# A fused attention and two-MLP kernel: the combined first weight stored with both parts side by side through one slotted tile, two attention units with longer query and key runs, and a new table of priorities

## The chip, the cores and the metric

The kernel runs on one core of a Trainium2 chip. A core has TensorE (matmuls; PE in the rows, its weight loads PEld), VectorE (DVE), ScalarE (ACT), GpSimd (POOL) and SyncE (SP), which here only issues transfers; 16 DMA engines carry them. The metric is the device time of one execution in microseconds, lower being better. Three runs of the kernel before took 761.55, 761.88 and 757.69 us, median 761.55.

## What is computed

Three parts follow each other, all in float32, with 4 batches of 576 tokens, 8 heads of 64 and a model width of 512.

```python
# attention: a coarse one on means over 4 tokens, repeated 4 times, plus a local one
out_d = sm_attn(mean4(q), mean4(k), mean4(v))
mask = np.abs(pos[:, None] - pos[None, :]) < 4
scores = np.where(mask, scale * q @ k.T, -1e9)
attn_out = np.repeat(out_d, 4, axis=2) + softmax(scores) @ v
# first MLP (w_k: 512x1024, w_v: 1024x512, w_r: 512x512), x_prev: x one token earlier
xk = mu_k * x + (1 - mu_k) * x_prev;  xr = mu_r * x + (1 - mu_r) * x_prev
x1 = sigmoid(xr @ w_r) * (np.maximum(xk @ w_k, 0) ** 2 @ w_v)
# second MLP (w_ch1: 512x2048, w_ch2: 2048x512)
xn = (x1 - mean) / np.sqrt(var + 1e-6) * g_ln
out = x1 + np.maximum(xn @ w_ch1, 0) @ w_ch2
```

The weights arrive as float64; each is read as pairs of 32-bit words and put together on the chip.

## The kernel before

**Precision.** Every large product is made of three matmuls on a high and a low part of each operand (`mm3`, L794 to L796): high times high, high times low, low times high. So each operand is split: a cast to the high part (`copy`, L391 on ScalarE or L392 on VectorE), then a subtraction for the low part (VectorE or POOL). A weight tile of 128x512 is loaded by `load_f32` (L405, 512 KB into a `w64` buffer, of which there are two), takes two passes on ScalarE (L411, L413) and two on VectorE (L418, L422), and is then split.

**Attention.** 16 units of two heads each; four units make a batch. A unit loads its queries and keys in one of several modes, set by `m0` to `m15` of the table: mode 0 with 128-byte runs (L508), modes 1 and 3 with two loads of 256-byte runs for each of q and k (L500), mode 2 with one load of 1536-byte runs for each (L493). In modes 1 to 3 TensorE turns the rows (tq, L571 to L577). Then come scores (sc, L645), the coarse scores (ds, L671), softmax on VectorE and ScalarE, transposes (tp, L723), the coarse output (up, L734) and the local output (pv, L764), and the sum into xT (L778), from which the first MLP takes its tokens. Values come in tiles v and vw (L517, L531).

**First MLP.** Six chunks of 384 tokens. For a chunk `prep` mixes neighbouring tokens and splits (tmu, xrh, xrl, xkh, xkl), `moe_r` makes the gate (psum tile psr, weights wr), `moe_k` the hidden columns (psk, weights wk) and `accumulate` the output (psv, weights wv). The chunks run between and after the attention units.

**Second MLP.** Three pairs of chunks. Each pair is a 2x2 block product by a Strassen-like scheme of seven products, for which the first weight is combined beforehand: `w1_combine` (L926) runs four times (two column groups g, two row blocks j), adds and subtracts quarter tiles a, and `put` (L938) splits each of the seven sums and stores high and low part to a scratch tensor s_dram. Before the change `put` takes for every part a buffer of its own: for g = 0 the seven tags sa1 to sa7 in turn, for g = 1 three tags alt0 to alt2 (L942); each part is stored by its own transfer (L950), 256 KB in runs of 512 bytes. Later `m2_product` (L1090) loads a 256 KB tile of s_dram for each product (sa, L1093); the first pair has a buffer for each of the seven products, the later pairs a ring of eleven (`ring`, L1183: seven sa tags and four wa), which they share with the tiles ta of the second weight (t_dram, L1365). The second weight is combined in `w2_combine` on tiles t (L903, L907). The normalised tokens go through z_dram and come back as zb (L1019), which VectorE transposes into raw (L1025); raw is summed and split into xn (L1082). Hidden columns of the later pairs are q (L1270 to L1288), split into hh and hl (L391, L903), and multiplied into pso.

**What sets the order.** The kernel is recorded as operations with an engine or a choice of engines, a cost, a priority and the buffers that they read and write. `Plan.order` gives each engine, step by step, the operation that can start first, by priority among equals; all engines and the SP queue then work in that order. The priorities, and the penalties `dve` and `pool` that tilt the choice between engines, come from the table PRM. Where TensorE is left without work before the first psv tile exists, warm-up matmuls (L449) are put in, one for each 0.14 us of the planner's own time.

## Time and profile before

| | before |
|---|---|
| profiled execution | 760.96 us, span 759.0 us |
| TensorE busy | 741.1 us (98%), 6248 matmuls |
| VectorE busy | 609.6 us (80%) |
| ScalarE busy | 466.5 us (61%) |
| POOL busy | 101.2 us (13%) |
| DMA | 180.33 MB, 81.6% of 16 engines in the core's queue |
| granted TensorE clock | full in all 40 slices |

Busy time of TensorE counts overlapping matmuls: one matmul stands with its latency (about 340 ns for 384 columns), and the next starts before it ends. A short wait can hide under that. A group's idle time is that of the engine just before its instructions, put down to what ended it.

### The profile page before, as it was taken

How to read it: one execution, taken by the hardware profiler on the slowest of the kernel's cores; microseconds unless marked ns; L12 is line 12 of the kernel's file. 1: busy time of each engine (PE TensorE's matmuls, PEld its weight loads, DVE VectorE, ACT ScalarE, POOL GpSimd, SP SyncE). 2: the span in 40 equal slices, each digit the busy share in tenths (PEclk: the TensorE clock that was granted, in tenths of full speed). 3: DMA queues.
4: the chain of work that ended last, by engine and by line, in shares of the span. 5: the costliest groups of instructions: out<-in, count | busy, mean ns of one | idle time of the engine just before them, and what ended most of it. 6: DMA issues, size and time to landing. Idle time of an engine off the chain costs nothing.

```text
span 759.0 us, 17473 instructions
## 1 busy us (share of the span) xinstructions
PE 741.1 (98%) x6248; PEld 659.9 (87%) x6248; DVE 609.6 (80%) x1304; ACT 466.5 (61%) x1073; POOL 101.2 (13%) x155
## 2 busy tenths in 40 slices
PE   9989999999999999999999999999989999999998
PEld 6767878888778888887988889989989999999998
DVE  6899999998985877978798698978578996334986
ACT  5788998987876766958853265452347452443552
POOL 3001112212100000001021022230101112110101
PEclk9999999999999999999999999999999999999999
DMA  9999696788585997883479979999997888986684
GB/s 185 180 199 187 166 198 135 164 176 172 171 190 188 279 309 222 232 271 122 126 252 364 268 255 354 352 341 334 310 321 237 244 253 282 382 255 205 210 263 154
DMA packets 198817, 180.33 MB, mean 238 GB/s; under 512 B 91968, under 2 KB 139468, under 8 KB 198732
## 3 DMA queue, kind: packets, MB, share of 16 engines
q1 hardware_dynamic: 198732, 179.23, 81.6%
q8 instruction: 50, 0.82, 0.5%
q14 instruction: 35, 0.29, 0.1%
HBM read 134.09 MB, written 45.09 MB: 236 GB/s over the span
## 4 chain that ended last, share of the span: by engine, by line
PE 73%; DMA 10%; DVE 8%; ACT 6%; issue 2%; SPq 0%; POOL 0%; DVEq 0%; POOLq 0%; ACTq 0%
PE pso L796 8%; PE pso L795 8%; PE pso L794 8%; PE psh L794 6%; PE psh L795 6%; PE psh L796 6%; PE psk L794 4%; PE psk L796 3%; PE psk L795 3%; DMA zb<-z_dram 3%; PE psv L794 3%; PE psv L796 3%; PE psv L795 3%; DMA w<-in_moe_w_k_dram 2%; PE warm L449 1%
## 5 line engine op out<-in xcount | busy, mean ns | idle before, releaser
L794 PE MATMUL psh<-xn,sa 128*128 128x384 f32 x336 | 114.2, 340 | 3.4 <-ACT q L1288 1.5
L795 PE MATMUL psh<-xn,sa 128*128 128x384 f32 x336 | 113.0, 336 | 0.0
L796 PE MATMUL psh<-xn,sa 128*128 128x384 f32 x336 | 112.8, 336 | 0.0
L391 ACT CAST hh<-q 128x384 fp32r<-128x384 f32 x109 | 56.2, 516 | 49.3 <-PE pso L795 44.2
L796 PE MATMUL pso<-ta,hl 128*128 128x256 f32 x300 | 84.6, 282 | 0.0
L795 PE MATMUL pso<-ta,hh 128*128 128x256 f32 x300 | 84.4, 281 | 0.0
L794 PE MATMUL pso<-ta,hh 128*128 128x256 f32 x300 | 84.2, 281 | 0.0
L794 PEld LDWEIGHTS psh<-xn,sa 128*128 128x128 f32 x336 | 63.0, 188 | 9.6 <-DVE c L1145 2.0
L795 PEld LDWEIGHTS psh<-xn,sa 128*128 128x128 f32 x336 | 63.1, 188 | 2.1
L796 PEld LDWEIGHTS psh<-xn,sa 128*128 128x128 f32 x336 | 63.1, 188 | 0.0
L903 DVE TENSOR_TENSOR hl<-q,hh 128x384 fp32r<-128x384 f32 x93 | 51.4, 557 | 9.6 <-ACT hh L391 8.5
L796 PEld LDWEIGHTS pso<-ta,hl 128*128 128x128 f32 x300 | 56.7, 189 | 0.0
L794 PEld LDWEIGHTS pso<-ta,hh 128*128 128x128 f32 x300 | 56.5, 188 | 0.0
L795 PEld LDWEIGHTS pso<-ta,hh 128*128 128x128 f32 x300 | 56.4, 188 | 0.0
L1288 ACT ACTIVATE q<-q 128x384 f32<-128x384 f32 x48 | 25.1, 525 | 45.6 <-DVE q L1278 24.5
L903 POOL TENSOR_TENSOR hl<-q,hh 128x384 fp32r<-128x384 f32 x19 | 19.8, 1047 | 152.8 <-ACT hh L391 152.7
L395 ACT ACTIVATE kr<-psk 128x384 f32<-128x384 f32 x46 | 22.4, 486 | 25.8 <-PE psk L796 23.9
L859 DVE TENSOR_TENSOR kl<-kr,kh 128x384 fp32r<-128x384 f32 x43 | 23.8, 554 | 17.4 <-ACT kr L858 17.0
L413 ACT ACTIVATE w<-w 128x512 uint32<-128x512 uint8 x52 | 34.9, 671 | 0.0
L907 DVE TENSOR_TENSOR q<-q,q 128x384 f32<-128x384 f32 x60 | 34.2, 577 | 0.0
L411 ACT ACTIVATE wf<-w 128x512 f32<-128x512 f32 x36 | 24.2, 672 | 16.1 <-DMA w<-in_moe_w_k_dram 5.3
L818 DVE SCALAR_TENSOR_TENSOR tmu<-xT,oms,tmu 128x384 f32<-128x384 f32 (+1 forms) x64 | 31.8, 513 | 2.7 <-ACT tmu L812 2.6
(585 smaller groups left out, 2103.4 us busy)
## 6 DMA issues: line engine op xcount, KB each, us to landing
sa<-s_dram SPq DMA_DIRECT2D x168, 256.0 KB, 4.6
ta<-t_dram SPq DMA_DIRECT2D x100, 256.0 KB, 3.2
w<-in_moe_w_ch_dram SPq DMA_DIRECT2D x32, 512.0 KB, 5.2
s_dram<-s SPq DMA_DIRECT2D x56, 256.0 KB, 4.0
t_dram<-t SPq DMA_DIRECT2D x32, 256.0 KB, 5.6
vw<-in_v_dram SPq DMA_DIRECT2D x62, 96.0 KB, 4.0
x_dram<-r SPq DMA_DIRECT2D x18, 256.0 KB, 2.7
x1t<-x_dram SPq DMA_DIRECT2D x6, 768.0 KB, 5.8
```

Of the source, the lines that this page charges most:

```text
L391: return [("ACT", c_act(n), lambda: nc.scalar.copy(dst(), src()), False), ("DVE", c_dve(n, True), lambda: nc.vector.tensor_copy(dst(), src ...
L395: return [("ACT", c_act(n, True), lambda: nc.scalar.activation(dst(), src(), AF.Relu), False), ("DVE", c_dve(n), lambda: nc.vector.tensor_ ...
L411: add("ACT", c_act(512), prio, lambda: nc.scalar.activation(f(), w64().bitcast(F32)[:, :, 1], AF.Abs, scale=2.0 ** -112), r=[w64], w=[f])
L413: add("ACT", c_act(512), prio, lambda: nc.scalar.activation(w64()[:, :, 0], w64().bitcast(U8).rearrange("p a (b c) -> p a b c", c=4)[:, :, ...
L794: nc.tensor.matmul(ps, lh, rh, start=start, stop=False, skip_group_check=more)
L795: nc.tensor.matmul(ps, lh, rl, start=False, stop=False, skip_group_check=more)
L796: nc.tensor.matmul(ps, ll, rh, start=False, stop=stop, skip_group_check=more)
L818: lambda t=t, o=o, n=n, prv=prv, kt=kt: nc.vector.scalar_tensor_tensor(t()[:, o:o + n], prv(), om[:, kt:kt + 1], t()[:, o:o + n], op0=ALU. ...
L859: add(either(C, lambda e: e.tensor_tensor(kl(), kr(), kh().bitcast(F32), op=ALU.subtract)), 0, prio, None, r=[kr, kh], w=[kl])
L903: add(either(n, lambda e: e.tensor_tensor(lo(), src(), hi().bitcast(F32), op=ALU.subtract)), 0, prio, None, r=r + wh, w=wl)
L907: add(either(n, lambda e: e.tensor_tensor(out(), a(), b(), op=op))[skip:], 0, prio, None, r=r, w=w)
L1288: return [("ACT", c_act(n), lambda: nc.scalar.activation(t(), t(), AF.Relu), False), ("DVE", c_dve(n, True), lambda: nc.vector.tensor_scal ...
```

## The change

1. The combined first weight goes through one tile `sring` of seven slots of 2 KB a partition. A `put` takes two neighbouring slots (three such pairs in turn, for both column groups), writes high and low part interleaved by 128 columns, and stores both with one transfer of 512 KB in runs of 1024 bytes. The sa tiles of the second MLP, and seven of the eleven places of the ring, become slots of the same tile.
2. Units 1 and 4 change from mode 1 to mode 2.
3. Nearly all other numbers of PRM are replaced. Two latencies of the planner become entries of the table, with the values that they had.

```diff
 PRM = dict(
-    thin=89.915, t0=-16.294, t1=-9.875, t2=6.158, t3=7.667, t4=48.796, t5=19.99, t6=6.382, t7=-23.592, t8=-0.47,
-    t9=-5.238, t10=-2.702, t11=0.12, t12=5.747, t13=-8.176, t14=-15.681, t15=-4.758, m0=2, m1=1, m2=0, m3=3, m4=1,
+    thin=89.915, t0=-1.975, t1=-8.717, t2=-1.015, t3=-1.866, t4=56.342, t5=38.532, t6=12.477, t7=24.291, t8=11.675,
+    t9=-14.459, t10=-2.748, t11=-6.438, t12=10.757, t13=10.235, t14=-8.667, t15=-6.125, m0=2, m1=2, m2=0, m3=3, m4=2,
...
-    n_put = [0, 0]
+    n_put = [0]
+    sring = Buf(w1tiles, [P, 7, 512], F32R, "sring", 1)
+
+    def slot(k, shape):
+        return View(sring, k, lambda t: t[:, k].rearrange("p (a b) -> p a b", b=shape[-1]) if len(shape) == 3 else
+                    t[:, k].rearrange("p (a b c) -> p a b c", b=shape[2], c=shape[3]))
...
         def put(i, src):
-            parts = []
-            for x in range(2):
-
-                tag = f"sa{n_put[0] % 7 + 1}" if g == 0 else f"alt{n_put[1] % 3}"
-                n_put[g] += 1
-                parts.append(Buf(w1tiles, [P, 512], F32R, tag, 1, f"s{i}"))
-            hi, lo = parts
-            add(copy(512, hi, src), 0, prio, None, r=[src], w=[hi])
-            add(either(512, lambda e: e.tensor_tensor(lo(), src(), hi().bitcast(F32), op=ALU.subtract)), 0, prio, None,
+
+            k = n_put[0] % 3
+            n_put[0] += 1
+            both = lambda t: t[:, 2 * k:2 * k + 2].rearrange("p a b -> p (a b)").rearrange(
+                "p (f x c) -> p f x c", x=2, c=P)
+            hi, lo = (View(sring, 2 * k + x, lambda t, x=x: both(t)[:, :, x]) for x in range(2))
+            raw = lambda: src().rearrange("p (f c) -> p f c", c=P)
+            add(copy(512, hi, raw), 0, prio, None, r=[src], w=[hi])
+            add(either(512, lambda e: e.tensor_tensor(lo(), raw(), hi().bitcast(F32), op=ALU.subtract)), 0, prio, None,
                 r=[src, hi], w=[lo])
-            for x, b in enumerate(parts):
-                add("SP", c_dma(P * 2048, 512), prio, lambda x=x, b=b: nc.sync.dma_start(
-                    out=s_dram[4 * g:4 * g + 4, SEQ.index(i), :, j, x].rearrange("f p c -> p f c"),
-                    in_=b().bitcast(F32).rearrange("p (f c) -> p f c", c=P)), r=[b], w=[(sd, (i, g, j, x))], lat=2.2)
+            add("SP", c_dma(P * 3000), prio, lambda: nc.sync.dma_start(
+                out=s_dram[4 * g:4 * g + 4, SEQ.index(i), :, j].rearrange("f p x c -> p f (x c)"),
+                in_=both(sring()).bitcast(F32).rearrange("p f x c -> p f (x c)")), r=[hi, lo],
+                w=[(sd, (i, g, j, x)) for x in range(2)], lat=2.2)
...
-        s = ring([P, 2, 2, P], "sa") if kept else Buf(w1tiles, [P, 2, 2, P], F32R, f"sa{i}", 1)
+        s = ring([P, 2, 2, P], "sa") if kept else slot(SEQ.index(i), [P, 2, 2, P])
...
-        return Buf(w1tiles, shape, F32R, *((f"sa{SEQ[k]}", 1) if k < 7 else ("wa", 4)), name)
+        return slot(k, shape) if k < 7 else Buf(w1tiles, shape, F32R, "wa", 4, name)
```

How the new table moves instructions is seen at three places. Lines are one to six higher in the changed kernel. The first place is the head of SP's queue (w_ are the w64 buffers, in_moe_w_k_dram and in_moe_w_r_dram the weights, kin and qin keys and queries, vraw the three vectors). Before:

```order
L405 DMA w_157<-in_moe_w_r_dram 128x1024
L493 DMA kin<-in_k_dram 96x2x384
L493 DMA qin<-in_q_dram 96x2x384
L405 DMA w_175<-in_moe_w_r_dram 128x1024
L500 DMA kin<-in_k_dram 96x6x64 x2
L500 DMA qin<-in_q_dram 96x6x64 x2
L1422 DMA vraw<-in_moe_mu_k_dram 4x128
L1422 DMA vraw<-in_moe_mu_r_dram 4x128
L1422 DMA vraw<-in_moe_g_ln_dram 4x128
```

After:

```order
L406 DMA w_157<-in_moe_w_k_dram 128x1024
L406 DMA w_171<-in_moe_w_k_dram 128x1024
L1428 DMA vraw<-in_moe_mu_k_dram 4x128
L1428 DMA vraw<-in_moe_mu_r_dram 4x128
L1428 DMA vraw<-in_moe_g_ln_dram 4x128
L494 DMA kin<-in_k_dram 96x2x384
L494 DMA qin<-in_q_dram 96x2x384
L494 DMA kin<-in_k_dram 96x2x384
L494 DMA qin<-in_q_dram 96x2x384
```

Two w_k weights and the vectors now stand ahead of unit 0's keys, where one w_r weight stood, and unit 1's keys and queries are one long-run load each. The four w_r weights come later and in the order 0 to 3; the last of them is row 30 of the queue, and was row 31.

The second place is the end of the attention on TensorE (tp, up and pv are the last unit's, psk and psv the first MLP's). Before:

```order
L734 MATMUL up<-pdT,vd 64x144 x4
L794 MATMUL psv_3964<-wv1h,kh 128x512
L795 MATMUL psv_3964<-wv1l,kh 128x512
L796 MATMUL psv_3964<-wv1h,kl 128x512
L794 MATMUL psv_3975<-wv1h,kh 128x512
L795 MATMUL psv_3975<-wv1l,kh 128x512
L796 MATMUL psv_3975<-wv1h,kl 128x512
L794 MATMUL psv_3985<-wv1h,kh 128x512
L795 MATMUL psv_3985<-wv1l,kh 128x512
L796 MATMUL psv_3985<-wv1h,kl 128x512
L764 MATMUL pv<-PT,vw 64x96 x12
L794 MATMUL psk<-xkh,wk01h 128x384
```

After:

```order
L795 MATMUL psk<-xkh,wk10h 128x384
L796 MATMUL psk<-xkl,wk10h 128x384
L797 MATMUL psk<-xkh,wk10l 128x384
L724 MATMUL tp<-isum,pd 72x2x64 x3
L795 MATMUL psk<-xkh,wk20h 128x384
L796 MATMUL psk<-xkl,wk20h 128x384
L797 MATMUL psk<-xkh,wk20l 128x384
L795 MATMUL psk<-xkh,wk30h 128x384
L796 MATMUL psk<-xkl,wk30h 128x384
L797 MATMUL psk<-xkh,wk30l 128x384
L735 MATMUL up<-pdT,vd 64x144 x4
L765 MATMUL pv<-PT,vw 64x96 x12
```

The last pv now follows its up at once, and the psv products that stood between them come behind it. Over the whole order 108 psr, 228 psk and 144 psv matmuls stand ahead of the last pv, which were 108, 240 and 162.

The third place is POOL during the first pair of the second MLP (t are tiles of the second weight, xn and raw those of the tokens). Before:

```order
L1082 TENSOR_TENSOR xn<-raw_6160,xn 128x384
L1082 TENSOR_TENSOR xn<-raw_6177,xn 128x384
L907 TENSOR_TENSOR t<-t 128x256 x2
L903 TENSOR_TENSOR t<-t 128x256
L907 TENSOR_TENSOR t<-t 128x256 x2
L903 TENSOR_TENSOR t<-t 128x256
L907 TENSOR_TENSOR t<-t 128x256 x2
L903 TENSOR_TENSOR t<-t 128x256
L907 TENSOR_TENSOR t<-t 128x256 x2
L903 TENSOR_TENSOR t<-t 128x256
L907 TENSOR_TENSOR t<-t 128x256
L903 TENSOR_TENSOR t<-t 128x256
```

After:

```order
L1088 TENSOR_TENSOR xn<-raw_5396,xn 128x384
L908 TENSOR_TENSOR t<-t 128x256 x5
L1088 TENSOR_TENSOR xn<-raw_6266,xn 128x384 x2
L1088 TENSOR_TENSOR xn<-raw_6282,xn 128x384
L908 TENSOR_TENSOR t<-t 128x256 x2
L904 TENSOR_TENSOR t<-t 128x256
L908 TENSOR_TENSOR t<-t 128x256
L1088 TENSOR_TENSOR xn<-raw_6266,xn 128x384 x2
L904 TENSOR_TENSOR hl<-q_7162,hh 128x384
```

Of 22 POOL instructions on t nine are left, and the other 13 are VectorE's.

## Rows read from the trace of the kernel before

**Rows 1.** Busy time of each engine over the whole span, from the page.

```profile
PE 741.1 (98%) x6248; PEld 659.9 (87%) x6248; DVE 609.6 (80%) x1304; ACT 466.5 (61%) x1073; POOL 101.2 (13%) x155
```

**Rows 2.** Busy time by stretch: span, then each engine in the order of the first row.

```profile
core 0: us, PE busy (x) PEld busy (x) DVE busy (x) ACT busy (x) POOL busy (x), PEclk, DMA share, GB/s
60.00:70.00 10.00, 9.74 (x44) 7.96 (x44) 9.62 (x21) 8.85 (x18) 1.56 (x4) 1.00 0.96 168
100.00:200.00 100.00, 99.50 (x1419) 82.14 (x1419) 93.43 (x210) 84.79 (x232) 23.71 (x45) 1.00 0.74 160
235.00:340.00 105.00, 102.65 (x519) 90.23 (x516) 79.52 (x162) 70.37 (x141) 2.27 (x2) 1.00 0.87 261
385.00:515.00 130.00, 128.62 (x634) 113.38 (x633) 109.63 (x233) 60.74 (x132) 28.12 (x32) 1.00 0.95 322
440.00:500.00 60.00, 60.00 (x296) 53.03 (x295) 53.88 (x107) 33.11 (x72) 16.34 (x19) 1.00 0.95 329
550.00:575.00 25.00, 22.74 (x133) 21.76 (x132) 18.52 (x42) 11.57 (x24) 1.06 (x2) 1.00 1.04 335
575.00:700.00 125.00, 125.00 (x886) 125.00 (x885) 83.32 (x165) 56.39 (x117) 17.20 (x16) 1.00 0.82 265
```

**Rows 3.** Groups of instructions: count, busy us, mean ns, idle us; the warm-up matmuls.

```profile
L449 PE MATMUL warm<-isum,identb 128*128 128x304 bf16 x135 | 23.1, 311 | 2.7 <-DVE identb L342 1.8 <-issue 0.9
```

**Rows 4.** Chain of waits, 0 to 70 us: start, us, what; two weight loads.

```profile
48.03 6.55 DMA w<-in_moe_w_r_dram
...
57.76 7.24 DMA w<-in_moe_w_k_dram
```

**Rows 5.** DMA queue, 0 to 57 us: packets, MB, share of 16 engines.

```profile
q1 hardware_dynamic: 26892, 10.59, 98.6%
```

**Rows 6.** The same queue from 600 to 680 us.

```profile
q1 hardware_dynamic: 12639, 23.01, 87.3%
```

**Rows 7.** Starts of neighbouring matmuls: chain from 225 us, then timeline at 548 us.

```profile
234.83 1.14 PE pv L764 x24
...
238.49 0.24 PE psv L795
238.72 0.23 PE psv L796
...
548.74 0.34 PE L796 MATMUL psh<-xn,sa 128*128 128x384 f32 x1
548.91 0.34 PE L794 MATMUL psh<-xn,sa 128*128 128x384 f32 x1
```

**Rows 8.** Groups by line: the two long weight passes on VectorE.

```profile
L418 DVE SCALAR_TENSOR_TENSOR wf<-wf,w 128x512 uint32<-128x512 uint32 x36 | 24.9, 695 | 9.8 <-ACT w L413 9.5
L422 DVE SCALAR_TENSOR_TENSOR wf<-w,wf 128x512 uint32<-128x512 uint32 x36 | 24.5, 681 | 0.2
```

**Rows 9.** The DMA queue from 241 to 337 us, while the first weight is stored.

```profile
q1 hardware_dynamic: 33795, 25.51, 88.3%
```

**Rows 10.** Line L950, the stores of the first weight, and who waited for them.

```profile
L950 SPq DMA_DIRECT2D s_dram<-s x56: 359/371/2511, 241.2 to 336.7; - x56
...
  DVE s L947: 2.9, 2
  ACT s L391: 1.8, 1
```

**Rows 11.** Groups on POOL from 385 to 515 us.

```profile
L907 POOL TENSOR_TENSOR t<-t 128x256 f32<-128x256 f32 x15 | 12.5, 836 | 45.8 <-DVE t L907 25.6 <-DVE w23l L903 9.3 <-DMA t_dram<-w27h 6.1
```

**Rows 12.** Groups on VectorE from 390 to 515 us.

```profile
L903 DVE TENSOR_TENSOR t<-t 128x256 fp32r<-128x256 f32 x22 | 9.9, 473 | 0.5 <-ACT t L391 0.4
L1082 DVE TENSOR_TENSOR xn<-raw,xn 128x384 fp32r<-128x384 f32 x13 | 8.6, 684 | 0.3 <-ACT xn L391 0.3
...
L907 DVE TENSOR_TENSOR t<-t 128x256 f32<-128x256 f32 x13 | 5.4, 416 | 0.0
```

**Rows 13.** Waits of VectorE from 540 to 575 us: total, times, longest.

```profile
DVE raw L1025 <- DMA zb<-z_dram: 4.6, 3, 1.9
```

23 lines of the change are left out of this document (12 added, 11 removed).

## The prediction

> **What bounds the kernel now.** I read the busy times of the page first: TensorE is busy for 741.1 of 759.0 us [rows 1], so only 18 us of plain idle are left. The table by stretch says where they lie [rows 2]. Behind 235 us TensorE carries dense products and is idle for 2.4 us (235 to 340), 1.4 us (385 to 515) and 2.3 us (550 to 575), and for none from 575 to 700. Before that it hides waits under other things: 135 warm-up matmuls fill 23.1 us [rows 3], and from 60 to 200 us VectorE is nearly full beside the attention units (9.62 of 10 us, then 93.4 of 100). The chain of waits of the first 70 us [rows 4] steps through weight loads: one of w_r takes 6.55 us from 48.03, one of w_k 7.24 us from 57.76; the DMA engines are full there (98.6% of 57 us [rows 5]). So the first 60 us wait on DMA, the attention stretch leans on VectorE, and behind 235 us there is little to win: 6.1 us in three stretches.
>
> The profiled execution took 760.96 us (span 759.0), 0.59 under the median of the runs, 761.55. The sum is made against 760.96.
>
> **The change, part by part.**
>
> *A. Queries and keys of units 1 and 4.* Before, each unit takes four loads of 256-byte runs, 576 runs each: 2304 packets. After, two loads of 192 runs of 1536 bytes: 384 packets, as unit 0 does now. Both units' loads stand on SP's queue ahead of the last w_r weight, before and after. The price of a packet: in the first 57 us 26892 packets took 98.6% of 16 engines [rows 5], 0.986 x 57 x 16 / 26892 = 33.4 ns at 394 bytes; from 600 to 680 us 12639 took 87.3%, 88 ns at 1.8 KB [rows 6]. 384 packets of 1536 bytes at 88 ns are 2.1 us of all engines. 2304 packets of 256 bytes are 4.8 us if each costs 33.4 ns, 3.1 us if the cost goes by bytes (21.7 ns). So a unit saves 1.0 to 2.7 us, the two 2.0 to 5.4 us. I take 3.0, nearer the low end, since 256 bytes lie under the 394 of the row. The engines are full there, so I count it on the path; if VectorE and ScalarE pace this stretch already, it is nothing. The first two queue places now hold two w_k weights ahead of unit 0's keys (one w_r before): 512 KB at the 10.59 MB per 57 us of this stretch, 2.8 us later for unit 0. It is the same bytes in another order, so the last weight does not move; I cost it at nothing, hidden by the weight loads, and 2.8 us if they are not what is waited for. TensorE's extra work (12 transposes of 128 columns per unit become 24 matmuls of 64, and 11 more fillers at 171 ns, 1.9 us [rows 3]) lies in time in which TensorE waits anyway.
>
> *B. The attention stretch.* The order puts 12 psk and 18 psv matmuls behind the last pv that stood ahead of it: 240 to 228 and 162 to 144 (psr 108 in both). At 0.17 us (384 columns) and 0.23 us (512) from one start to the next [rows 7] that is 2.0 + 4.1, about 6.2 us. VectorE has 462 instructions up to the last write of xT instead of 464, eight fewer of the two long weight passes among them (695 and 681 ns [rows 8]), which shorter ones partly replace: I estimate 2 us less. If TensorE paces the stretch (99.5 of 100 us busy), moving its work costs nothing. If VectorE paces it, attention ends 2 us earlier with 6.2 us more left behind: +4.2. I take +1.0, nearer TensorE, whose row is fuller.
>
> *C. The combined first weight.* 56 stores of 512-byte runs become 28 of 1024 bytes; the bytes are the same, the packets fall from 28672 to 14336. From 241 to 337 us a packet cost 0.883 x 96 x 16 / 33795 = 40 ns [rows 9]. The engine time saved is between nothing (cost by bytes) and 14336 x 40 ns / 16 = 36 us (cost by packets), but no step of TensorE waits for a transfer there: what shows is that VectorE waited 2.9 us and ScalarE 1.8 us for such stores to leave a buffer [rows 10]. The second half-weight had three single buffers, now three pairs serve all, so these waits should shrink. TensorE's idle time in 235 to 340 is 2.4 us, the most this can give. The strided halves cost VectorE and ScalarE nothing that a row shows; the bound is one 681 ns pass of 512 columns [rows 8], by which the first part's store now waits for the second. I take -1.0, between +0.7 and -2.4. The 28 issues that SP loses are waited for by nobody.
>
> The Trainium skill's page "DMA: Bandwidth & Descriptors" (Specifications) puts line rate at 512 bytes and up, by which C would win no transfer time and the sum stand 1.0 us higher; no run so far shows this part alone. The skill's "Perfetto Trace Analysis" (DMA Optimizations) says that split transfers may let some start sooner, which speaks against joining two stores: by it the sum would be 1.7 us higher.
>
> *D. Second weight of the last part.* Of the 22 POOL instructions on the t tiles (15 shown [rows 11]) 13 go to VectorE, of those on xn four, on raw two. VectorE's rows for them are 473 and 416 ns (t) and 684 ns (xn) [rows 12]; with raw counted like xn that is 13 x 0.45 + 6 x 0.68 = 9.9 us, most of it in 385 to 515, where VectorE is busy 109.6 of 130 us and TensorE idles 1.4 [rows 2]. On average it fits, with 10 us to spare. Cost between 0 and +3.8 (rival 2); I take +0.5.
>
> *E. The last pair of chunks.* Its zb loads stop VectorE for 4.6 us in three stops [rows 13], and TensorE stands 2.3 us in 550 to 575 [rows 2], since VectorE's transposes of zb are queued ahead of the sums that free PSUM. In the new order the 16 transposes stand two or three such sums later, their loads two or three ring loads later; there are five sums for seven ring loads, so the loads gain about one product. I take -1.0, between 0 and -2.3.
>
> The sum: -3.0 + 1.0 - 1.0 + 0.5 - 1.0 = -3.5, so 760.96 - 3.5 = **757.5 us**, 0.5% under the median of the runs. Everything else of the new table reorders work without changing its amount.
>
> **Rivals.**
> 1. *The first part gives more.* For it: fillers and waits there are the largest pool, and the four w_r weights now come in the order in which psr uses them, so that its first product can start with five weights landed instead of eight. A at its full 5.4, C at 2.4, E at 2.3, B and D nothing: -10.1, **751 us**. Against it: from 60 to 70 us VectorE and ScalarE are busy 9.62 and 8.85 of 10 us [rows 2], and all eight weights must still pass them. Chance 0.27.
> 2. *Slower: VectorE becomes the bound.* The 9.9 us of D all fall on the column steps of 440 to 500, where it is busy 53.9 of 60 us [rows 2]: 63.8, a lag of 3.8. PSUM is then freed late and each product behind it waits. With VectorE pacing the attention stretch too, B is +4.2 and unit 0's later keys +2.8, and A, C and E give nothing: 760.96 + 10.8 = **772 us**. It decides once VectorE passes 59 of those 60 us. Against it: the moved work spreads over more steps than that. Chance 0.15.
> 3. *Nothing that is moved is waited for.* The short packets hide behind the weight passes of ScalarE and VectorE, the stores were covered, B's gain and loss cancel: **761 us**. Chance 0.18.
> My forecast has 0.40.
>
> **Numbers.** The range runs from rival 1 less 5 us, since the new order of the first 235 us may gain more than its rows can price, to short of rival 2: 746 to 769. About 1% (7.6 us) is what a measurement of this kernel, whose runs spread over 757.69 to 761.88, can tell from no change. Under 753.9: nearly all of rival 1 and a little of the forecast, 0.29. Over 769.2: most of rival 2, 0.13. Between: 0.58.
>
> **What would show it.** A: the steps on w_r and w_k at 48 and 58 us come some 3 us earlier, and the last pv, now ending at 236 us [rows 7], comes near 231. B: no more idle time of TensorE in 100 to 200 than now. C: no wait of VectorE or ScalarE for stores of s_dram; TensorE's idle time in 235 to 340 near 1.4 us. D: VectorE over 115 of 130 us in 385 to 515, TensorE idle under 2. E: zb stops VectorE for under 3.5 us. I am wrong if the last pv comes no earlier, or if TensorE loses over 3 us between 385 and 515.

## The result: 0.6% slower, and the profile after

The changed kernel takes 764.52 us (median of 10 runs, 761.54 to 766.50), the kernel before 758.99 in the same measurement (757.69 to 763.52): ratio 1.0061, 95% interval 1.0038 to 1.0085. I had predicted 757.5 us, a small gain; it is a loss of 5.5 us, inside the range (746 to 769) and inside 1%, on the wrong side of zero. The profiled execution took 765.51 us. The one shown of before (760.96, from which the sum started) lies 2.0 us over that kernel's median of 758.99, this one 1.0 over its own, so the two executions differ by 4.6 us, and the two spans by 4.7.

From the page and the table by stretch, in the columns of [rows 1, 2]; here with the first 60 us, in which the kernel before has 54.28 (x964), 41.57 (x964), 47.10 (x109) for the first three engines, at a granted clock of 1.00:

```profile
PE 745.8 (98%) x6331; PEld 665.5 (87%) x6331; DVE 614.0 (80%) x1323; ACT 469.7 (62%) x1079; POOL 78.3 (10%) x129
```
```profile
0.00:60.00 60.00, 52.95 (x857) 40.17 (x858) 42.10 (x100) 36.92 (x96) 11.90 (x39) 0.97 0.85 168
100.00:200.00 100.00, 98.95 (x1432) 80.97 (x1430) 92.74 (x210) 81.88 (x225) 15.92 (x34) 1.00 0.80 165
235.00:340.00 105.00, 102.37 (x518) 88.76 (x517) 82.37 (x163) 75.80 (x153) 2.66 (x2) 1.00 0.85 284
385.00:515.00 130.00, 129.19 (x640) 115.30 (x639) 110.13 (x245) 68.38 (x153) 13.86 (x14) 1.00 0.90 299
440.00:500.00 60.00, 59.52 (x294) 52.86 (x293) 49.54 (x111) 29.80 (x63) 7.62 (x8) 1.00 0.96 312
550.00:575.00 25.00, 23.98 (x146) 23.46 (x145) 16.02 (x40) 11.79 (x24) 1.02 (x1) 1.00 0.96 288
```

TensorE's idle time over the span is what it was: 17.9 us in both (763.7 - 745.8 and 759.0 - 741.1). So the 4.7 us by which this span is longer stand as busy time: the page has 83 more matmuls (6331 against 6248), 72 of them transposes and 11 fillers, and a stretch at half clock is in it too. Idle time has moved to the front. In the first 60 us TensorE idles 7.1 us (5.7 before) and VectorE has got through 42.1 us of work instead of 47.1; from 385 to 515 and from 550 to 575 us TensorE idles less than before (0.8 us instead of 1.4, and 1.0 instead of 2.3). The last psv product, which closes the first part, marks how much is lost on the way. From the timeline of TensorE (start and duration in us, engine, line), before and after:

```profile
388.51 0.39 PE L796 MATMUL psv<-wv7h,kl 128*128 128x512 f32 x1
```
```profile
397.20 0.40 PE L797 MATMUL psv<-wv7h,kl 128*128 128x512 f32 x1
```

8.7 us are lost up to here, and 4.0 won back behind it (763.7 - 397.2 = 366.5 us to the end, against 370.5). Of the 8.7, 1.7 stand at the end of the last pv (237.6 us against 236.0) and 7.0 between it and the last psv product. Of what is lost early the chain of waits (start, us, what) shows the largest piece at once, between two matmuls of the same transposition group:

```profile
14.41 0.55 PE sc L646 x43
14.96 1.30 PE tq L572 x26
16.26 3.80 issue
20.06 0.54 PE tq L572 x6
20.60 0.54 PE warm L450 x2
```

"issue" is a stop in which TensorE waits for nothing that the profile names: no semaphore, no transfer of data. Two stretches around it, in the columns above: TensorE does nothing for 3.7 us, and from 20.7 to 24.0 us its granted clock is 0.50, the lower of its two levels (1.2 of 2.4 GHz).

```profile
16.30:20.00 3.70, 0.00 (x0) 0.00 (x0) 0.00 (x0) 0.68 (x1) 0.00 (x0) 1.00 1.12 213
20.70:24.00 3.30, 3.30 (x30) 2.49 (x28) 1.82 (x3) 0.76 (x2) 0.00 (x0) 0.50 0.88 99
```

The other rows that answer to those of before. The DMA queue from 0 to 57 us [rows 5], with 5,918 packets fewer, and the last pv of the chain [rows 7]:

```profile
q1 hardware_dynamic: 20974, 9.61, 84.7%
```
```profile
236.58 1.04 PE pv L765 x24
```

Who waited for the stores of the first weight [rows 10]; the POOL group on t from 385 to 515 us [rows 11]; the VectorE groups on t from 390 to 520 us, 5 us more than in [rows 12] since all comes later; and VectorE's wait for zb from 540 to 580 us [rows 13]:

```profile
L955 SPq DMA_DIRECT2D s_dram<-sring x28: 359/370/1332, 243.8 to 330.2; - x28
...
  ACT sring L392: 5.6, 5
  DVE sring L393: 1.0, 2
```
```profile
L908 POOL TENSOR_TENSOR t<-t 128x256 f32<-128x256 f32 x8 | 6.4, 804 | 90.5 <-DMA t_dram<-t 51.9 <-DVE t L908 33.7 <-ACT b L392 4.9
```
```profile
L904 DVE TENSOR_TENSOR t<-t 128x256 fp32r<-128x256 f32 x31 | 13.1, 426 | 1.4 <-ACT t L392 1.3
L908 DVE TENSOR_TENSOR t<-t 128x256 f32<-128x256 f32 x24 | 10.0, 417 | 0.0
```
```profile
DVE raw L1031 <- DMA zb<-z_dram: 2.9, 1, 2.9
```

### The profile page after: what moved, and what is told of

Read it like the earlier page. It is cut to its first block, busy times and chain, and to the rows that moved or that the text cites. A ratio compares the mean times of both kernels' runs of the same rounds, so it can differ in the third digit from the quotient of the medians.

```text
span 763.7 us, 17526 instructions
## 1 busy us (share of the span) xinstructions
PE 745.8 (98%) x6331; PEld 665.5 (87%) x6331; DVE 614.0 (80%) x1323; ACT 469.7 (62%) x1079; POOL 78.3 (10%) x129
## 4 chain that ended last, share of the span: by engine, by line
PE 77%; DVE 11%; DMA 7%; issue 2%; ACT 2%; SPq 0%; POOL 0%; DVEq 0%; POOLq 0%; ACTq 0%
PE pso L797 8%; PE pso L795 8%; PE pso L796 8%; PE psh L795 7%; PE psh L796 7%; PE psh L797 7%; PE psk L795 4%; PE psk L797 3%; PE psk L796 3%; PE psv L795 3%; PE psv L796 3%; PE psv L797 3%; PE warm L450 3%; DMA s_dram<-sring 1%; PE psr L795 1%
## 5 line engine op out<-in xcount | busy, mean ns | idle before, releaser
L795 PE MATMUL psh<-xn,sring 128*128 128x384 f32 x254 | 85.9, 338 | 0.8 <-DVE c11l L1120 0.5
L796 PE MATMUL psh<-xn,sring 128*128 128x384 f32 x254 | 85.5, 337 | 0.0
L797 PE MATMUL psh<-xn,sring 128*128 128x384 f32 x254 | 85.4, 336 | 0.0
L904 DVE TENSOR_TENSOR hl<-q,hh 128x384 fp32r<-128x384 f32 x100 | 55.7, 561 | 10.4 <-ACT hh L392 9.6
L795 PE MATMUL pso<-sring,hh 128*128 128x256 f32 x195 | 54.8, 281 | 0.0
L797 PE MATMUL pso<-sring,hl 128*128 128x256 f32 x195 | 54.8, 281 | 0.0
L796 PE MATMUL pso<-sring,hh 128*128 128x256 f32 x195 | 54.8, 281 | 0.0
L795 PEld LDWEIGHTS psh<-xn,sring 128*128 128x128 f32 x254 | 47.7, 188 | 4.3 <-ACT u L388 1.1
L796 PEld LDWEIGHTS psh<-xn,sring 128*128 128x128 f32 x254 | 47.7, 188 | 1.9
L797 PEld LDWEIGHTS psh<-xn,sring 128*128 128x128 f32 x254 | 47.7, 188 | 0.0
L797 PEld LDWEIGHTS pso<-sring,hl 128*128 128x128 f32 x195 | 36.8, 189 | 0.0
L796 PEld LDWEIGHTS pso<-sring,hh 128*128 128x128 f32 x195 | 36.8, 189 | 0.0
L795 PEld LDWEIGHTS pso<-sring,hh 128*128 128x128 f32 x195 | 36.7, 188 | 0.0
L813 ACT ACTIVATE tmu<-xT,vecs 128x384 f32<-128x384 f32 (+1 forms) x54 | 27.5, 533 | 6.4 <-DVE xrl L823 2.3
L419 DVE SCALAR_TENSOR_TENSOR wf<-wf,w 128x512 uint32<-128x512 uint32 x36 | 24.6, 683 | 7.1 <-ACT w L414 7.1
```

The lines of the kernel that those rows point to most:

```text
L419: lambda: nc.vector.scalar_tensor_tensor(fu(), fu(), 3, w64()[:, :, 0], op0=ALU.logical_shift_left, op1=ALU.bitwise_or),
L795: nc.tensor.matmul(ps, lh, rh, start=start, stop=False, skip_group_check=more)
L796: nc.tensor.matmul(ps, lh, rl, start=False, stop=False, skip_group_check=more)
L797: nc.tensor.matmul(ps, ll, rh, start=False, stop=stop, skip_group_check=more)
L813: add([("ACT", c_act(n, ap=1), lambda t=t, o=o, n=n, cur=cur, kt=kt: nc.scalar.mul(t()[:, o:o + n], cur(), mu[:, kt:kt + 1]), False), ("DV ...
L904: add(either(n, lambda e: e.tensor_tensor(lo(), src(), hi().bitcast(F32), op=ALU.subtract)), 0, prio, None, r=r + wh, w=wl)
```

## The experiments

Each kernel was timed beside the kernel before on the same chip; ratios are to that kernel. "Changed kernel" is the one above.

### 1. The order of the first loads

*Keys first, in the changed kernel* (the first nine loads of SP's queue in the old order):
```
+ sp = [i for i in seq if self.ops[i].ways[self.ops[i].way][0] == "SP"]
+ head = [sp[x] for x in (0, 5, 6, 1, 7, 8, 2, 3, 4)]
+ seq = head + [i for i in seq if i not in head]
```


> The changed kernel with one edit: on SP's queue the first nine loads stand as in the kernel before (one weight, keys and queries of unit 0, one weight, keys and queries of unit 1, the three vectors) instead of both weights and the vectors first. Every other engine keeps its order. Theory 1 (late keys): the first transposes start near 6.7 us instead of 9.5, all of the early chain comes 2.8 us earlier, 764.5 - 2.8 = 761.7 us. Theory 2 (TensorE waits for its own instructions: its 3.8 us stop at 16.3 us, in which it waits for nothing that the profile names, ends when an instruction piece lands): the piece lands as late as before, TensorE only reaches the stop sooner and stands there up to 6.6 us, the time stays at 764.5 within 1. Theory 3 (the order of everything else in the first 70 us): under 1 us of change, with the first transposes early all the same.

Measured: 766.30 us, ratio 1.0113 (1.0088 to 1.0138): slower still. With the keys first the three vectors come last, and TensorE's program has their transposition (vps) near its head; the chain shows what it did:

```profile
5.01 7.48 DMA vraw<-in_moe_g_ln_dram
...
12.53 0.28 PE vps L1435
```
```profile
8.40:12.40 4.00, 0.20 (x2) 0.00 (x0) 0.00 (x0) 0.66 (x1) 0.00 (x0) 0.81 1.22 188
12.60:20.50 7.90, 7.90 (x63) 5.52 (x64) 2.89 (x6) 3.70 (x8) 0.00 (x0) 0.50 1.00 203
```

TensorE waits 4 us for the vectors, and then works 8 us at half clock. None of the three theories had this. The kernel is no test of the keys; it is one of what a stop of TensorE costs here: the stop, and the half clock behind it.

*Keys late, in the kernel before* (the same edit with `(0, 3, 8, 9, 10, 1, 2, 4, 5, 6, 7)`):

> The kernel before with one edit: SP issues both first weights and the three vectors ahead of the keys and queries of units 0 and 1, as the changed kernel does. Every other engine keeps its order. Theory 1 (late keys): 759.0 + 2.8 = 761.8 us, and the first transposes near 9.5 us. Theory 2: the instruction stops (1.1 us at 21.9 us in the kernel before) grow only if the loads that share the engines at that moment change; 759 to 760. Theory 3 and my prediction, which costed this at nothing: 759.0 within 1.

Measured: 758.19 us beside 758.17, ratio 1.0004 (0.9986 to 1.0022). TensorE waits 0.85 us for the keys and begins its first transposes at 7.5 us, 0.9 later than in the trace of before, not 2.8; nothing is lost:

```profile
2.69 4.79 DMA kin<-in_k_dram
...
7.52 1.21 PE tq L574 x24
```

A delay of 2.8 us is not tested by this. But in the changed kernel the chain has no wait for keys at all ahead of its first transposes; fillers and the vectors' transposition stand there:

```profile
1.78 6.59 PE warm L450 x30
8.37 0.16 PE vps L1432
8.53 1.01 PE warm L450 x7
9.54 1.14 PE tq L572 x24
```

So late keys cost the kernel before nothing, and are not what the changed kernel waits for. Theory 1 falls.

### 2. The long runs

*Short runs in the changed kernel*: units 1 and 4 load 256-byte runs again, in two loads per tensor, and transpose 128 columns at a time.

> The changed kernel with one edit: units 1 and 4 take their queries and keys in 256-byte runs again, by one pair of loads per tensor in the place of the one load, and by 6 transposes of 128 columns instead of 12 matmuls of 64 per tensor. Order of all engines else unchanged. My term A: these loads cost 3.0 us more, 767.5. Theory that the long runs themselves cost time (24 more TensorE instructions a unit, copies out of PSUM that write every sixth element): 2 to 4 us less, 761 to 762.5. Theories 1 and 3: no more than 1 us either way.

Measured: 761.84 us, ratio 1.0045 (1.0021 to 1.0069); the changed kernel stands at 1.0061 (1.0038 to 1.0085). Undoing the long runs does not cost 3 us; if anything it wins 1 to 3.

*Long runs in the kernel before*, one load for each head in the places of the old loads, with the transposes and copies that they need:
```
+ swap = n in (1, 4)
+ runs = mode == 2 or swap
...
+         out=dst()[:96, 384 * hp:384 * hp + 384],
+         in_=src[b, 2 * u + hp].rearrange("(p c) d -> p (c d)", c=6),
```


> The kernel before with one edit: units 1 and 4 take queries and keys in 1536-byte runs (one head per load, in the places of the old loads) and transpose them by 12 matmuls of 64 columns per tensor. Order of all engines unchanged. My term A, 2.0 to 5.4 us less, 3.0 taken: 756. Theory that the long runs themselves cost time: 2 to 4 us more, 761 to 763. If neither is on the path: 759.0 within 1.

Measured: 760.28 us beside 758.17, ratio 1.0038 (1.0014 to 1.0062): 2 to 3 us lost where term A had 3 won. Its trace has a stop in the same transposes (waits of TensorE to 60 us: total, times, longest), with the clock at 1.00 behind it; the trace of before has two such stops up to 60 us, 2.0 us together, so this trace alone does not say that stops are what was lost:

```profile
PE tq L575 <- issue: 2.4, 1, 2.4
```

The extra transposes are more than the prediction counted. These are groups of the kernel before in mode 2 (L571, units 0 and 7, as set by m0 and m7) and in mode 1 (L577, units 1 and 4), on the keys, and the one group that the changed kernel has for all four units:

```profile
L571 PE MATMUL tq<-isum,kin 96*64 96x96 f32 x48 | 2.4, 250 | 0.0
L577 PE MATMUL tq<-isum,kin 96*128 96x96 f32 x12 | 1.8, 262 | 1.2 <-ACT ups L387 1.1
```
```profile
L572 PE MATMUL tq<-isum,kin 96*64 96x96 f32 x96 | 5.9, 272 | 0.0
```

A unit has 6 records for the keys in mode 1 and 24 in mode 2: the 12 matmuls of 64 columns stand as two records each, the 6 transposes of 128 as one. For queries and keys of two units that is 72 matmuls more, 144 records with the weight loads, where the prediction has 24 matmuls (and the expectation of the split transposes in experiment 5 has 48).

### 3. What the stop is

Count the records of TensorE: matmuls, weight loads and its waits for semaphores. In all nineteen traces the nameless stops of over 0.3 us before 60 us fall at the same places of the program, whatever the instruction there: the 450th, the 706th, the 1218th, the 1474th, all of the form 450 + 256 k. The page of either kernel has 50 packets of 16 KB on a queue of kind "instruction", and TensorE has 12,825 records before and 12,982 after: 256 to 260 for each packet. Each such stop ends 1.3 to 1.7 us after one of these packets has landed; in the changed kernel one runs from 17.29 to 18.77 us, alone of its queue from 17.2 to 18.8:

```profile
q8 instruction: 1, 0.02, 5.8%
```

I read this as TensorE waiting for its own instructions, which come as packets too; no other reading that I tried ties a stop to a count of records. Worked out from the traces (us): when TensorE passes record 194, when the first packet starts and lands, when record 450 runs, the time from record 194 to the one before record 450, and from that one's start to record 450 (a stop, with the one record in it).

```
                        194    packet         450    194 to 450   stop
before                 11.13  12.64-13.60    16.19      4.9        0
before, long runs      11.58  15.36-16.46    17.91      3.7        2.7
changed                13.03  17.29-18.77    20.06      3.0        4.0
changed, short runs    12.54  15.96-17.19    18.75      4.0        2.3
changed, split stores  11.77  12.49-13.94    15.59      3.0        0.8
changed, lighter       13.19  17.92-19.18    20.51      3.0        4.3
changed, plus rows      9.51  10.93-12.48    14.99      5.5        0
```

The packet starts 0.7 to 4.7 us behind record 194 in these (0 to 4.7 in all nineteen) and takes 1.0 to 1.6; where there is a stop, record 450 runs 1.3 to 1.7 us after it has landed. That delay is a matter of the execution: "changed" and "changed, split stores" (experiment 6) have the same program up to 241 us and differ by 3.5 us in it. What the program decides is how long TensorE is busy with the 256 records in between. The long runs put 24 short records per tensor where 6 were: in the kernel before they cut this cover from 4.9 to 3.7 us, in the changed order from 4.0 to 3.0. Whether it is then caught, and for how long, is up to the execution. In the new order the clock fell to 0.50 within 1 us behind such a stop in four of five traces (changed, short runs, and the two of the changed kernel in experiment 4; not with split stores), for 3 to 7 us; in the old order it stayed at 1.00 up to 30 us in every trace.

The head of the program differs from execution to execution as well. The 30 fillers above took 6.59 us in the trace of the changed kernel and 5.32 in that with split stores, the same instructions:

```profile
1.78 5.32 PE warm L450 x30
```

### 4. Lighter loads

*Values of units 0 and 1 in contiguous runs of 3 KB*, in the changed kernel:
```
+ if n < 2:
+     m = (g1 - g0) * D
+     nc.sync.dma_start(
+         out=dst.rearrange("p g d -> p (g d)")[:, D * g0:D * g1],
+         in_=bass.AP(tensor=a.tensor, offset=a.offset, ap=[[m, 32], [1, m]]))
+     return
```
These loads fetch as many bytes, but other values; only the time is read. The same holds for the two kernels after this one.


> The changed kernel with one edit that takes away DMA packets and nothing else: the eight value loads of units 0 and 1 that fill the windowed value tiles read contiguous runs of 3 KB per partition in place of 12 runs of 256 bytes (the same 96 KB each, so the values are the wrong ones; the attention of the first two units is not computed rightly). Order of all engines unchanged. Theory 2 (TensorE's stop at 16.3 us is the wait for its own instructions, a 16 KB piece that stands behind these loads in full DMA engines): the piece starts by 15 us instead of 17.3, the stop of 3.8 us shrinks under 1.5, the granted clock does not fall behind it, and everything behind comes 3 to 5 us earlier: 759.5 to 761.5. Theory 4 (24 more TensorE instructions a unit and the copies cost the time by themselves): the stop may go, the rest of the chain does not move by more than 1 us, 763.5 to 765. Theory 3 (the order of the rest of the first 70 us sets it): within 1 us of 764.5 too.

Measured: 763.42 us, ratio 1.0067 (1.0045 to 1.0088): no gain. In its trace the first packet lands at 14.0 us and the stop at record 450 is gone, as theory 2 had it; but TensorE, now early, is caught at record 706, and the half clock follows:

```profile
20.68 2.45 issue
23.13 0.33 PE sc L652 x17
```
```profile
23.50:26.20 2.70, 2.70 (x17) 1.63 (x16) 2.67 (x9) 1.59 (x4) 0.13 (x2) 0.50 0.81 161
```

*All short runs of units 0 to 3 made contiguous*, in the changed kernel and in the kernel before:

> The changed kernel, in which all loads of units 0 to 3 with runs under 1 KB (values, queries and keys) take contiguous runs of 1.1 to 3 KB instead: the same bytes in far fewer packets, other values (the attention of these four units is not computed rightly). Order of all engines unchanged. Theory 2, widened (the loss of the first 235 us is TensorE waiting for its own instructions behind short packets, and the half clock that follows such stops): no instruction stop over 0.5 us and no granted clock under 1.00 before 60 us, the 36th psr product near 70 us instead of 77, and 4 to 6 us less in all: 758.5 to 760.5. If the order of the work in the new table is what costs (theory 3), the stops may go and the time stays over 762.5.

> The kernel before with the same edit of the same units' loads (contiguous runs, the same bytes, other values; the attention of units 0 to 3 is not computed rightly). Order of all engines unchanged. Its instruction stops sum to some 2 us (1.1 at 21.9 and 1.1 at 43.6 us) and its clock never falls, so theory 2 expects 1.5 to 2.5 us less than the kernel before, 756 to 757.5, and the lightened changed kernel to come within 3 us of it, where the two stand 5.5 apart now. Theory 3 expects the two lightened kernels to stay 5 to 6 us apart.

Measured: 761.72 us, ratio 1.0041 (1.0020 to 1.0061), and 756.61, ratio 0.9975 (0.9956 to 0.9995). By the medians both are 2 to 3 us faster than without the edit, the first with an interval that overlaps the changed kernel's, and they stay 5.1 apart. Packets up to 57 us fell from 20974 to 9102 in the first, and the stop of 4.1 us at record 450 is there all the same. So the short packets alone are not what holds the instruction packet up: theory 2 in that form falls. The kernels' distance stays open here, since the stops stay.

### 5. Instructions alone

*120 more instructions at the head of TensorE's program, no more work*: 69 small matmuls stand in for nine of the first 17 fillers, 60 matmuls and 60 weight loads more. This moves every end of an instruction piece by 120 records and leaves all else in its order.
```
+ def tiny(n):
+     for _ in range(n):
+         nc.tensor.matmul(warm()[:32, :32], identb[:32, :32], isumb[:32, :32], start=True, stop=True)
...
- add("PE", 4.5, -20.0, warm_up, w=[warm])
+ add("PE", 4.5, -20.0, lambda: (tiny(69), warm_up(8)), w=[warm])
```


> The changed kernel with 120 more instructions at the head of TensorE's program and no more work: nine of its first seventeen warm-up matmuls give way to 69 small ones of 32 columns, each with its weight load. All other instructions and all loads are those of the changed kernel. In fourteen traces TensorE's stops fall at the same places of its program, every 256 instructions (the 450th, the 706th, ...), and end 1.3 to 1.7 us after a 16 KB piece of the instruction queue has landed; such a piece starts 0 to 4.7 us after TensorE has passed the instruction 256 earlier. In the changed kernel TensorE covers the 256 instructions up to the 450th in 2.9 us, in the kernel before in 5.0, so it is caught in more executions. With 120 instructions ahead, the first such stretch lasts 5 us or more and the next 5.3. Theory 2 in this form: stops under 1.5 us in sum up to 30 us, no fall of the granted clock there, and 2 to 5 us less: 760 to 762.5. If the stops are a symptom and not a cause: 764.5 within 1.

Measured: 760.12 us (758.76 to 761.39), ratio 1.0015 (0.9999 to 1.0030), against 1.0061 for the changed kernel: 3.5 us by the ratios, 4.4 by the medians, won by instructions that do nothing. The spread of its runs is 2.6 us where the changed kernel's is 5.0. The chain through the same place, now whole, and the stretch (clock 1.00, TensorE without idle time):

```profile
15.48 1.47 PE tq L576 x32
16.95 0.36 PE warm L450 x2
```
```profile
8.00:24.00 16.00, 16.00 (x363) 11.78 (x362) 10.91 (x24) 10.46 (x26) 0.26 (x4) 1.00 1.12 188
```

*The same in the kernel before*, as a control:

> A control for after_plus_rows: the same 120 instructions at the head of TensorE's program in the kernel before. If they helped the changed kernel by moving the ends of its instruction pieces, they do little here, where the stretches between those ends are long already (5.0, 4.4, 8.4 us without them; 5.1, 5.4, 7.9 with them): 757.5 to 759.5 beside 758.9. If small matmuls at the head help by themselves (the clock, the first wait), the gain is that of the changed kernel: 754.5.

Measured: 760.15 us beside 758.73, ratio 1.0020 (0.9996 to 1.0044): no gain, if anything 1 us lost. The small matmuls don't help by themselves. Its one trace has no nameless stop up to 60 us (2.0 us in the trace of before) and is the fastest of its twelve runs (756.59 us), so one trace cannot tell how often such stops come.

*The transposes of units 1 and 4 in halves, loads as before*:
```
+ if n in (1, 4):
+     for hp in range(2):
+         o = P * (c0 + c) + 64 * hp
+         nc.tensor.matmul(tqv()[64 * hp:64 * hp + 64, c], src()[:96, o:o + 64], ident[:96, :96],
+                          start=True, stop=True)
```


> The kernel before with its own loads, in which units 1 and 4 transpose each 128-column piece by two matmuls of 64 columns, as the long runs need it: 24 more TensorE matmuls a unit (48 more instructions with their weight loads) and nothing else. The long runs together with these took 0.4% more (760.3 against 758.2). If the instructions are what costs there: 760 to 761.5, with a stop of some 2 us before 20 us. If the loads or the copies of every sixth element cost it: 758.6 within 1.

Measured: 760.62 us beside 758.95, ratio 1.0026 (1.0002 to 1.0050): some 2 us, barely clear of nothing and most of what the long runs cost. It adds TensorE's time as well as instructions: by the rows in experiment 2 two units take 4.8 us in mode 2 and 3.3 in mode 1 (L571 and L577, keys 2.4 and 1.8, queries 2.4 and 1.5), an estimate of 1.5 us for the two. Its one profiled execution (span 755.6) was not caught at record 450, so the cost stands on the times alone, and what part of it is the fetch is not shown.

### 6. Term C: the combined first weight

*Two stores instead of one, from the slotted tile*, in the changed kernel:
```
+ for x in range(2):
+     nc.sync.dma_start(
+         out=s_dram[4 * g:4 * g + 4, SEQ.index(i), :, j, x].rearrange("f p c -> p f c"),
+         in_=both(sring()).bitcast(F32)[:, :, x])
```


> The changed kernel with one edit: each joint store of the slotted tile is issued as two again (512-byte runs, one for each half, one behind the other from the same place on SP's queue). Order of all engines else unchanged. By my term C, in which the joint store wins: 1 us slower, 765.5, with VectorE's and ScalarE's waits for these stores longer than 6.6 us. If transfers there are hidden: 764.5 within 1, the last psk at the same place behind the last pv to 0.5 us. If joining is what hurts: those waits fall under 5 us and the time by up to 1 us.

Measured: 763.53 us, ratio 1.0069 (1.0044 to 1.0094) against 1.0061: no difference that shows. TensorE idles 2.3 us from 235 to 340 (2.6 with the joint store), so transfers are hidden there.

*The slotted tile with the old table*, and *with four pairs of slots* (`[P, 8, 512]` and `n_put[0] % 4` for `[P, 7, 512]` and `% 3`):

> The kernel before, its own table of numbers, with the slotted tile and the joint stores of the combined first weight alone; all engines' orders are those of before up to the first store at 241 us and are planned anew behind it. My term C took -1.0, between +0.7 and -2.4: 758.0 by it. If the joint store only makes both halves wait for each other and for a pair to come free, as the changed kernel's longer waits for these stores say (4.7 us before, 6.6 after): 759 to 760, TensorE's idle time in 235 to 340 up by 0.7 us. If the structure has no part in it: 759.0 within 1.

> The kernel before with the slotted tile and joint stores, in which the stores now go round four pairs of slots instead of three (a tile of eight slots). The order up to 241 us is that of before. With three pairs this structure took 0.6% more than the kernel before (762.7). If the scarce pairs are what costs (ScalarE and VectorE waited 4.4 us for such stores and VectorE 6.7 us for ScalarE's halves): 758.5 to 760.5, and those waits halved. If it is something else, the order that is planned around the new structure for one: 762 to 763.5.

Measured: 762.72 us, ratio 1.0058 (1.0035 to 1.0082), and 759.40, ratio 0.9997 (0.9981 to 1.0013). The structure alone cost 4 us under the old settings, and one more pair took that away. Three pairs first, four pairs second (235 to 340 us, columns as above):

```profile
235.00:340.00 105.00, 100.98 (x487) 87.37 (x486) 76.41 (x154) 70.04 (x142) 3.33 (x2) 1.00 0.82 266
```
```profile
235.00:340.00 105.00, 104.21 (x519) 90.31 (x516) 78.24 (x157) 71.88 (x147) 4.35 (x4) 1.00 0.79 268
```

TensorE's idle time goes from 4.0 to 0.8 us. VectorE's wait for ScalarE's halves falls from 6.7 to 2.7 us; the direct waits for the stores do not (4.4 and 6.2), so I take it that the pair as a whole comes free too late, and not that a transfer is slow; no run separates the two.

*Four pairs in the changed kernel* (with the 120 instructions, planned anew behind 241 us):

> The changed kernel with the 120 instructions of after_plus_rows and four pairs of slots for the stores of the combined first weight instead of three; planned anew behind 241 us. If the third pair's wait costs the changed kernel what it costs the old settings (3 us): 757 beside 760.1. If its own settings already hide it, as they did with the old early part (757.7 and 756.5, 1.2 us): 759 to 760.

Measured: 762.45 us, ratio 1.0047 (1.0026 to 1.0067): 2 us more than with three, against both expectations. The waits for the stores fell (4.6 to 3.2 us), TensorE's idle time there hardly (2.3 to 2.0). With its own settings the changed kernel loses nothing to the third pair; what the new plan lost instead was not followed up.

### 7. The late part, and a version that beats both

*The new settings behind 240 us with the old tiles*; *with the slotted tile*; *with four pairs*. All three keep the old table and loads up to 241 us; from the changed kernel they take wc, wcs, wcg, w2, w2s, sld, dp, tp, tp0 and tps of PRM, and its charges for VectorE and POOL behind 240 us of the planner's time:
```
- x = at + cost + self.LOAD[eng]
+ late = at > 240.0
+ x = at + cost + ({'DVE': 0.244, 'POOL': 0.072}.get(eng, 0.0) if late else self.LOAD[eng])
```


> The kernel before with its own tiles and stores, and only the changed kernel's settings for the second weights and the last part and its charges for VectorE and POOL behind 240 us: my terms D and E without A, B and C. The order is that of before up to some 390 us. From the two traces the stretch behind 390 us gained 3.9 us (8.7 late at 389 us, 4.8 at the end): 759.0 - 3.9 = 755. By my terms D and E (+0.5 and -1.0): 758.5. If the gain was only the slack of a late start: 759 within 1.

> The slotted tile and joint stores, with the old table for everything up to 241 us (short runs, old order of the loads; the same order as the kernel before on every engine there) and, behind it, the changed kernel's settings for the combined weights, the second weights and the last part, and its charges for VectorE and POOL. If the changed kernel lost 8.7 us in the first 390 us and won 3.9 us back behind them, as the two traces say, this one keeps the gain without the loss: 759.0 - 3 = 756, between 755 and 757.5. If the late gain is only slack that the late start gave (waits that shrink because the loads had more time), nothing is won: 758 to 760.

> The best of what was found, meant to beat both: the old table and loads up to 241 us, the slotted tile with four pairs for the stores instead of three, and the changed kernel's settings behind 240 us. The same with three pairs took 757.7 beside 758.4 for the kernel before. If the fourth pair is worth what it is with the old settings (3 us): 754 to 756. If the new settings already hide the third pair's wait: 757.5 within 1.

Measured: 758.93 us, ratio 1.0001 (0.9987 to 1.0015); 757.69, ratio 0.9995 (0.9968 to 1.0021); 756.52, ratio 0.9971 (0.9953 to 0.9988). The late settings are worth nothing on the old tiles (TensorE idles 4.7 us in 385 to 515) and 0.6%, over 4 us, on the slotted ones (1.0058 to 0.9995). The second kernel has the slotted tile and the late settings of the changed one, but not its loads, long runs and other entries of PRM, nearly all of which set priorities of the attention and the first MLP: 0.9995 (0.9968 to 1.0021) against 1.0061 (1.0038 to 1.0085). So the loss of the changed kernel, some 5 us, comes with these. The last kernel is 0.3% faster than the kernel before and 0.9% faster than the changed one, by the two ratios; its late stretches:

```profile
235.00:340.00 105.00, 103.45 (x497) 89.15 (x496) 78.94 (x160) 73.24 (x149) 4.34 (x4) 1.00 0.78 264
385.00:515.00 130.00, 129.65 (x647) 116.36 (x646) 109.58 (x239) 67.84 (x148) 16.18 (x18) 1.00 0.97 327
```

## Why the prediction was wrong, step by step

**The step that failed is A**, and in it two sentences. "The engines are full there, so I count it on the path": the packets fell (by A's count of 3,840 for the two units, and by 5,918 up to 57 us), the engines went from 98.6 to 84.7% busy, and nothing came earlier. The chain shows why. The nine traces with the old order and the old loads (in one of them the first loads in another order) all have one or two weight loads of 4.8 to 7.2 us in the chain between 43 and 72 us [rows 4]. With the long runs put into the kernel before there is none, and VectorE and ScalarE stand in the same place:

```profile
53.23 0.61 DVE wf L418
53.86 0.70 DVE wf L422
54.59 0.37 ACT wk30h L391
```

It is the same in the changed kernel, up to its first gate product, which comes at 63.3 us (59.6 in the trace of before):

```profile
58.36 1.29 DVE e L701
59.65 0.38 DVE xT L779
60.05 0.61 ACT tmu L813
...
63.25 0.50 PE psr L795
```

That is A's own condition, "if VectorE and ScalarE pace this stretch already, it is nothing", and -3.0 was taken all the same. The runs then came out worse than nothing: the long runs put into the kernel before cost 0.38% (0.14 to 0.62), and the bounds 0 to -5.4 left out a loss.

The loss lies in the other sentence, "TensorE's extra work ... lies in time in which TensorE waits anyway". The extra work was counted too low (24 matmuls instead of 72, experiment 2), and its instructions have to be fetched, while the prediction priced no instruction but by the time it runs. Splitting the transposes costs 0.26% with the old loads, time and fetch together; moving the ends of the pieces gives the changed kernel 0.46% back (experiment 5), which I put down to the fetch, since no work but nine fillers went. The signs were in the trace of before, unread: its chain had stops named "issue" that I passed over, and [rows 3] has 0.9 us of such idle time.

The sentence on unit 0's late keys, "I cost it at nothing", held in the kernel before (1.0004).

**B** (+1.0, between 0 and +4.2) was asked whether TensorE or VectorE paces 60 to 235 us, and was taken too near TensorE. A and B together were to give 2.0 us; at the last psv product the trace is 8.7 late. The last pv ends at 237.6 us and not near 231, which I had named as a sign of being wrong, and the 6.2 us of products that were moved behind it come on top. Single traces differ: the last pv ends between 231.5 and 236.3 us in the eleven traces of the old order and between 232.6 and 239.8 in the eight of the new one. What holds in all of them is the rest: from there to the last psv product it is 151.9 to 155.0 us in the old order and 159.0 to 160.8 in the new one. So 6.2 us of TensorE's work were taken out of the stretch and it ended no earlier, also where no nameless stop is left up to 60 us (234.1 and 234.6 us with the 120 instructions, 233.6 in the kernel before with them). The amount of TensorE's work did not set its end, and the bound of +4.2 was nearer than +1.0; what paced it behind 63 us was not followed up. TensorE's idle time in 100 to 200 us doubled (0.5 to 1.05 us), where it was to stay.

How much of the 8.7 us experiment 5 takes away can't be read from its trace. Its last psv product starts at 393.24 us, but the trace with split stores, of the changed kernel's own program up to 241 us, has it at 393.37. The medians are what shows the gain.

**C** (-1.0, between +0.7 and -2.4): ScalarE and VectorE wait 6.6 us for the stores instead of 4.7, in more and shorter waits, not less; TensorE's idle time in the stretch is 2.6 us instead of 2.4. "Three pairs serve all, so these waits should shrink" was wrong: the first half had seven single buffers, and three pairs are six. Under the old settings that costs 4 us (1.0058), well outside the bounds. The joint store is neither gain nor loss (experiment 6); the Trainium skill's "DMA: Bandwidth & Descriptors" (Specifications), which puts line rate at 512 bytes and up, agrees with that.

**D** (+0.5) was better than forecast: VectorE took the work (x31 and x24 on t, 22 and 13 before), its busy time in 385 to 515 went from 109.63 to 110.13 us only, and TensorE's idle time fell from 1.4 to 0.8. In 440 to 500 us VectorE is busy 49.5 of 60, so rival 2 was far off.

**E** (-1.0): zb stops VectorE for 2.9 us instead of 4.6, and TensorE's idle time in 550 to 575 falls by 1.2. The wait behaved as foreseen, in size too; no run has E alone, so its worth in time is not shown. Behind the last psv, where D and E lie, 4.0 us are won back between the two traces instead of 0.5. By experiment 7 the late settings need the slotted tile: they are worth nothing on the old tiles, and the slotted tile without them loses.

In the sum, A to C were to give 3.0 us up to the last psv and cost 8.7; D and E were to give 0.5 behind it and gave 4.0, by one trace of each kernel. By the ratios of experiment 7, A and B with the rest of the new table for the first part, for which -2.0 was taken, came out at some +5, and the slotted tile with the late settings, for which -1.5 was taken, at about nothing (0.9995). That the range held the time was its width, 23 us, and not the sum. No rival had the fetch of instructions; rival 2, the one on the slower side, had the bound for B that is nearer to these traces, but its larger part, VectorE in 440 to 500 us and a wait for late keys, did not occur.

## What to carry to other kernels

Before a shorter transfer is counted on the path, see what stands next to it there: here VectorE's queue was as long as the loads. Look at the stops named "issue" before pricing added instructions, and count these in the trace and not in the source: where many short matmuls run back to back, an instruction costs its fetch too, and the count of instructions between two pieces is a resource like a buffer. To see whether such a stop costs time, put idle-time fillers of another count at the head of the program, which moves the ends of the pieces and changes little else, and read the medians. A change of structure and a new table of numbers should be tried apart: here the structure cost 4 us with the old numbers, the numbers gave nothing with the old structure, and together they gained.

## What the runs showed of the hardware

- TensorE's program comes in during the execution: 50 packets of 16 KB on the instruction queue, each for some 256 records. From record 194 to the start of the first of them 0 to 4.7 us passed, by the execution and not by the number of data packets around it (4.3 us in the changed kernel, 4.7 with its packets up to 57 us cut from 20974 to 9102). The Trainium skill's page "Runtime: NRT & Kernel Launch" (Instruction fetch mechanics) has TensorE's instructions refilled in blocks of 16 KiB, 256 instructions each, while the kernel runs, and calls the cost of a boundary mostly hidden. The traces agree on size and count; on the cost they differ, with stops of up to 4.1 us at such boundaries, and the measurement decides.
- A float32 matmul of 64 columns against the identity stands as two matmul records and two weight loads, a transpose of 128 columns as one of each (24 records for 12 matmuls and 6 for 6 transposes, experiment 2).
- Behind a stop of 2.0 to 4.1 us the granted clock fell to 0.50 for 3 to 7 us in some executions and stayed at 1.00 in others (2.4 us in the kernel before with long runs; 2.1 with split stores). A wait of 4 us for data, 8 us into the program, was followed by 8 us at half clock.
- The same program up to 241 us ended its last pv at 237.6 us in one execution and at 234.3 in another (split stores). By record 194 the two stand 1.3 us apart, from the fillers at the head; their nameless stops up to 60 us sum to 5.0 and 2.6 us.
